# Gate work of an expert six units later, a third buffer for float32 weight parts, and row gathers placed behind GpSimd's subtractions

## Chip, cores and metric

One core of one Trainium2 chip runs the whole program as one kernel. The metric is the time of an execution on the device in microseconds (us); three executions of the kernel before gave 1203.83, 1204.12 and 1204.78 us, and their median is the time before.

## The reference

Three layers, one after the other, all in float32. The first takes the real part of a two-dimensional Fourier transform of x, four sequences of 2496 rows by 256. The second assigns the 9984 rows greedily to 8 experts of 1248 places each and applies the expert's two matrices. The third is a second mixture of experts, whose gate picks one expert for each row:

```python
# layer 2, N, D, E, F = 9984, 256, 8, 1024
for idx in argsort(-(x @ w_gate).flatten()):      # the best pairs first
    tok, e = idx // E, idx % E
    if assigned[tok] < 0 and counts[e] < N // E:
        assigned[tok] = e; counts[e] += 1
out[assigned == e] = relu(x[assigned == e] @ w1[e]) @ w2[e]
# layer 3
e_idx  = argmax(x @ w_gate2); gate_w = softmax(x @ w_gate2)[e_idx]
eom    = sigmoid(x @ w_output_gate)[e_idx]
out[e_idx == e] = gate_w * eom * (relu(x[e_idx == e] @ w1b[e]) @ w2b[e])
```

## The kernel before

**Numbers.** Every float32 matrix product is made of three float16 matmuls: a value is split into a high and a low half ("hi" and "lo"), and hi·hi, hi·lo and lo·hi are summed. So each weight block and each activation is split by two instructions: ScalarE (ACT) writes the high half, and VectorE (DVE) or GpSimd (POOL) subtracts it from the float32 value.

**Stages.** The Fourier transform and the choice of the first expert take the start. Then follow layer 2's experts 0 to 7, one after the other, in the trace from about 160 to 733 us, and layer 3 from about 754 us to the end. The change concerns layer 2 alone. Experts are chosen one at a time by a bisection on DVE with small matmuls (tiles `s_msk`, `sp`, `r`), which runs beside the expert before.

**One expert of layer 2.** Its 1248 rows come in three chunks (384, 384 and 480 rows). `hidden` (L898) makes, for each of 8 blocks of 128 hidden features, six matmuls into a PSUM tile `ph` (three buffers), then the relu on ACT (`ht`, L904), then the low half: on DVE (L910), or, for odd blocks in experts 0 to 4, ACT writes `hf` (L907) and POOL subtracts (L908). `out_block` (L915) makes 24 matmuls for 128 rows into `py` (two buffers), and ACT copies it to `yr` (L921). TensorE (PE) takes the hidden part of chunk c+1 before the output part of chunk c.

**Side work.** A class `Flow` emits the PE units of the experts in order and counts a clock of units, each about 1 us of PE's work. Between units it steps side generators when their due time has come: `yield 4.0` means "four units later". The order of the program on PE follows this. On the other engines a scheduler sets the final order, and `issue_after(x)` makes an instruction stand behind x on its queue. The generators that matter here:

- `prepare` (L1041): loads the six float32 weight blocks of an expert (`wf`, 0.5 MB each, issued on SP, the queue of SyncE; four stage buffers), finds the places of its rows (`places`, DVE L669 to L686, PE `px`), gathers the rows with ten indirect DMAs (`xg`, POOL L873; one buffer), and transposes the first chunk.
- `weights` (L1061): splits four of these blocks (ACT L783, DVE L785 or POOL L788).
- `gates` (L1074): uses the last two blocks, the second matrix transposed (`moe_w2t`), to multiply layer 3's gate columns into the expert's second matrix. It works in four steps of 256 columns: splits into `wt` (L799, one buffer), waits `GG` units, 12 matmuls (L809), two writes into `wh` (L815).
- `keep2` (L1082): prepares layer 3's weights while layer 2 runs. For each of 8 experts it takes four parts of 0.5 MB: SP loads a part into one of two float32 buffers (tiles `g_0`, `g_1`), ACT and DVE split it into `wp` (L1102, L1103), SP stores it (`wsd`, L1104), then the load of the part after next is issued. One part is due every 7 units (`KY`); a counter of experts (`KEEP`) holds it back. Parts are numbered 0 to 31 here.
- `rest` and `route` (L924): after an expert, layer 3's gate for its rows, the store `yd`, and ten indirect DMAs that scatter entries into a list (`lst`, POOL L985), four units apart.

SP's queue is in order: the loads of `wf`, which wait for a stage buffer, the store `yd`, which waits for the route, `keep2`'s loads and its stores all stand in it, one behind the other.

Of the kernel before, what the change touches and what calls it, by code (L numbers as in the profile page):

```python
# [723 lines left out]
GA = 0  # L724
G0 = 2.5
GN = 256
GG = 8.0
RY = 5.0
GY = 2.0
SY = 2.5  # L730
XY = 2.0
KY = 7.0
# [103 lines left out]
class Moe1:  # L836
    CH = ((0, 3), (3, 3), (6, 4))

    def __init__(self, tc, nc, a, xd, yd, lst, wsd, sel, pools, consts, bufs):
        self.tc, self.nc, self.a, self.xd, self.yd, self.lst, self.sel = tc, nc, a, xd, yd, lst, sel  # L840
        self.P = pools
        self.c = consts
        p = pools["keep"]
        self.base = p.tile([128, 8], F32, name="m_base")
        nc.vector.tensor_copy(self.base, consts["eoff"])
        self.wg = p.tile([128, 2, 2, 16], F16, name="m_wg")
        self.scat = []
        self.W = Weights(nc, pools["wts"], pools["stage"], a["moe_w1"], a["moe_w2"], a["moe_w2t"])
        self.wsd, self.bufs = wsd, bufs
        self.W2 = Weights(nc, pools["wts"], pools["stage"], a["moe2_w1"], a["moe2_w2"])  # L850
# [10 lines left out]
    def load(self, k):  # L861
        e = self.nc.sync.value_load(self.sel.ei[0:1, k:k + 1], min_val=0, max_val=7)
        return self.W.load(e)

    def gather(self, k):
        nc = self.nc
        idx = self.sel.idx[k]
        xg = self.P["xg"].tile([128, 10, D], F32, name="xg")

        def steps():  # L870
            for t in range(10):
                m = 128 if t < 9 else 96
                nc.gpsimd.indirect_dma_start(out=xg[:m, t], out_offset=None, in_=self.xd,  # L873
                                             in_offset=bass.IndirectOffsetOnAxis(ap=idx[:m, t:t + 1], axis=0))
                yield
        return xg, steps()

# [20 lines left out]
    def hidden(self, xt, n, wh, k):  # L898
        nc = self.nc
        ht = self.P["ht"].tile([128, 2, 8, 512], F16, name="ht")  # L900
        for fk in range(8):
            ph = self.P["psum"].tile([128, 512], F32, name="ph", bufs=3)
            ffn1_unit(nc, xt, wh[0], fk, n, ph[:, :n])
            self.act = nc.scalar.activation(ht[:, 0, fk, :n], ph[:, :n], AF.Relu)  # L904
            if fk % 2 and fk // 2 < HP[k]:
                hf = self.P["work"].tile([128, 480], F32, name="hf", bufs=HFB)
                nc.scalar.activation(hf[:, :n], ph[:, :n], AF.Relu)  # L907
                nc.gpsimd.tensor_sub(ht[:, 1, fk, :n], hf[:, :n], ht[:, 0, fk, :n])  # L908
            else:
                nc.vector.scalar_tensor_tensor(ht[:, 1, fk, :n], ph[:, :n], 0.0, ht[:, 0, fk, :n],  # L910
                                               op0=OP.max, op1=OP.subtract)
            yield n * 6 / 2400.0
        self.ht = ht
# [10 lines left out]
    def route(self, yr, k):  # L924
# [54 lines left out]
        nc.vector.tensor_copy(pi, px)  # L979
        nc.vector.tensor_add(self.base, self.base, pr[:, 80:88])  # L980
        self.counted = k
        ent = self.lst.rearrange("r (s w) -> (r s) w", w=2)
        for t in range(10):
            m = 128 if t < 9 else 96
            s = nc.gpsimd.indirect_dma_start(out=ent, in_=en[:m, t], in_offset=None,  # L985
                                             out_offset=bass.IndirectOffsetOnAxis(ap=pi[:m, t:t + 1], axis=0))
            for o in self.scat:
                self.tc.declare_no_dep(s.ins, o.ins, reason="every row has a place of its own")
            self.scat.append(s)
            yield 2.0 if k == 6 else 8.0 if k == 7 else 4.0  # L990

    def ffn(self, k, flow):

        wh = self.ws.pop(k)
        xg, xt = self.xgs.pop(k)
        yr = self.P["yr"].tile([128, 10, YW], F32, name="yr")
        self.nc.gpsimd.memset(yr[96:128, 9], 0.0)
        hts, nxt = {}, []

        def unit(d):  # L1000
            flow.unit(d)
            while nxt and nxt[0][0] <= 0:
                if next(nxt[0][1], 1):
                    nxt.pop(0)
                    self.cut += 1
                break
            if nxt:
                nxt[0][0] -= 1

        for c in range(4):  # L1010
            if c < 3:
                cur = xt
                if c < 2:
                    xt, st = self.xt(xg, c + 1)
                    nxt.append([3, st])
                for d in self.hidden(cur[0], cur[1], wh, k):
                    unit(d)
                hts[c] = self.ht
            else:
                self.tail = k  # L1020
            if c > 0:
                flow.until(lambda: self.gated >= k)
                t0, nt = self.CH[c - 1]
                for t in range(nt):
                    m = min(128, CAP - (t0 + t) * 128)
                    for d in self.out_block(hts[c - 1], t0 + t, t * 128, m, wh, yr):
                        unit(d)

        def rest():
            yield from self.route(yr, k)  # L1030
            self.routed = k
        flow.add(rest(), 1.0, prio=PR)
# [8 lines left out]
    def prepare(self):  # L1041

        for k in range(8):
# [4 lines left out]
                self.sel.placed = k  # L1048
            yield lambda: self.sel.placed >= k
            xg, steps = self.gather(k)  # L1050
            for t, _ in enumerate(steps):
                yield 0.0 if t < 4 else GY
            yield lambda: self.tail >= k - 1
            xt, steps = self.xt(xg, 0)
            for _ in steps:
# [1 line left out]
            self.xgs[k] = (xg, xt)  # L1057
            yield lambda: k in self.ws
            self.ready = k

    def weights(self):  # L1061

# [11 lines left out]
    def gates(self):  # L1074

        for k in range(8):
            yield lambda: k in self.gs and self.at >= (k - 1 if k else GA)
            for d in self.W.gate(*self.gs.pop(k), self.wg, self.P["psum"]):
                yield d or 0.0 if k else G0
            self.gated = k  # L1080

    def keep2(self):  # L1082
# [1 line left out]
        nc = self.nc  # L1084
        yield lambda: self.at >= KEEP[0]
        h = self.P["wts"].tile([128, 4, 2, 1024], F16, name="wp", bufs=1)
        fs = [self.bufs[q % 2].rearrange("p a b -> p (a b)")[:, :1024] for q in range(4)]

        def load(e, q):
            with self.tc.issue_after(self.W.at.ins):  # L1090
                self.W2.part(fs[q], slice(e, e + 1), q)

        load(0, 0)
        load(0, 1)
        for e in range(8):
            if e and KEEP[e] > self.at:
                yield lambda: self.at >= KEEP[e]
            else:
                yield KY
            for q in range(4):  # L1100
                with self.tc.issue_after(self.act.ins):
                    nc.scalar.activation(h[:, q, 0], fs[q], AF.Copy, scale=64.0)  # L1102
                nc.vector.scalar_tensor_tensor(h[:, q, 1], fs[q], 64.0, h[:, q, 0], op0=OP.mult, op1=OP.subtract)  # L1103
                nc.sync.dma_start(self.wsd[e, :, q], h[:, q])  # L1104
                if e < 7 or q < 2:
                    load(e + q // 2, (q + 2) % 4)
                if q < 3:
                    yield KY
            self.kept = e

    def run(self, flow, m2):
        self.cut = 0
        self.gated = -1
        self.counted = self.kept = -1
# [430 lines left out]
```

## Time and profile before

| what | value |
|---|---|
| median of three executions | 1204.12 us (1203.83 to 1204.78) |
| profiled execution, its own time | 1203.47 us |
| profiled execution, span from first to last instruction | 1201.7 us |
| mean granted clock of TensorE | 0.976 of full speed |
| busy share of the span | PE 93%, DVE 61%, POOL 41%, ACT 37% |

The span and the profiled execution's own time are 1.8 us apart, and the median of the three runs is 0.65 us above the profiled execution. A granted clock of 1 is 2.4 GHz, 0.5 is 1.2 GHz. In the rows below, `L824` is line 824 of the program; `py<-wh,ht` names the output tile and the inputs without buffer numbers; `x6` stands for six such instructions in a row.

### The profile page before, as it was taken

How to read it: one execution, taken by the hardware profiler on the slowest of the kernel's cores; microseconds unless marked ns; L12 is line 12 of the kernel's file. 1: busy time of each engine (PE TensorE's matmuls, PEld its weight loads, DVE VectorE, ACT ScalarE, POOL GpSimd, SP SyncE). 2: the span in 40 equal slices, each digit the busy share in tenths (PEclk: the TensorE clock that was granted, in tenths of full speed). 3: DMA queues.
4: the chain of work that ended last, by engine and by line, in shares of the span. 5: the costliest groups of instructions: out<-in, count | busy, mean ns of one | idle time of the engine just before them, and what ended most of it. 6: DMA issues, size and time to landing. Idle time of an engine off the chain costs nothing.

```text
span 1201.7 us, 24544 instructions
## 1 busy us (share of the span) xinstructions
PE 1119.0 (93%) x9823; PEld 821.8 (68%) x9823; DVE 729.9 (61%) x1786; ACT 440.8 (37%) x936; POOL 498.4 (41%) x471
## 2 busy tenths in 40 slices
PE   7998879979898989899798999999999999999998
PEld 4653546756667657567485767766766799999997
DVE  5866779897978977867456574434334343434343
ACT  3423334263452734345354443222223122222221
POOL 3825351468373781433306045643332334343331
PEclk8999989999999999989899999999999999999999
DMA  7834722243341571686838458444343366788782
GB/s 257 334 122 157 264 80 88 61 128 65 106 90 64 155 182 56 150 271 155 239 129 244 162 134 295 139 157 153 119 172 114 119 250 234 273 311 331 308 332 92
DMA packets 80036, 212.96 MB, mean 177 GB/s; under 512 B 11850, under 2 KB 48986, under 8 KB 69168
## 3 DMA queue, kind: packets, MB, share of 16 engines
q1 hardware_dynamic: 65360, 180.46, 44.5%
q0 software_dynamic: 14560, 30.91, 8.5%
q8 instruction: 78, 1.28, 0.5%
q14 instruction: 38, 0.31, 0.1%
HBM read 162.22 MB, written 50.42 MB: 177 GB/s over the span
## 4 chain that ended last, share of the span: by engine, by line
PE 28%; issue 23%; DVE 16%; POOL 10%; DMA 9%; ACT 2%; POOLq 0%; SPq 0%; DVEq 0%; ACTq 0%
PE py L832 14%; PE ph L824 9%; DMA g<-moe_w 6%; DMA out<-ot,tbrow 3%; POOL xg L1336 3%; POOL out L1381 2%; POOL g L1336 2%; DVE s_msk L525 2%; DVE ht L910 2%; PE px L693 1%; POOL xg L873 1%; DVE wp L1103 1%; PE pt L890 1%; POOL lst L985 1%; PE sp L531 1%
## 5 line engine op out<-in xcount | busy, mean ns | idle before, releaser
L832 PEld LDWEIGHTS <-ht 128*128 128x128 f16 (+1 forms) x3912 | 380.6, 99 | 61.3 <-issue 6.0
L824 PE MATMUL ph<-xt,wh 128*128 128x384 f16 (+4 forms) x2352 | 386.1, 316 | 26.9 <-DVE ht L910 14.8
L832 PE MATMUL py<-wh,ht 128*128 128x272 f16 (+2 forms) x3264 | 393.8, 277 | 4.2 <-ACT yr L921 4.2
L824 PEld LDWEIGHTS <-wh 128*128 128x128 f16 x2352 | 211.2, 99 | 148.8 <-issue 38.8
L1368 ACT ACTIVATE ht<-ph 128x512 f16<-128x512 f32 x166 | 99.1, 597 | 315.8 <-PE ph L824 315.8
L1369 DVE SCALAR_TENSOR_TENSOR ht<-ph,ht 128x512 f16<-128x512 f32 x166 | 114.8, 691 | 126.7 <-ACT ht L1368 126.7
L985 POOL DMA_INDIRECT lst<-r_en,r_pi x80 | 87.5, 1094 | 145.5 <-DVE r_pi L979 89.5
L904 ACT ACTIVATE ht<-ph 128x384 f16<-128x384 f32 (+1 forms) x192 | 98.4, 516 | 85.0 <-PE ph L824 76.9
L1381 POOL DMA_INDIRECT out<-ot,tarow x54 | 54.5, 1010 | 158.8 <-DVE ot L1380 152.1
L873 POOL DMA_INDIRECT xg<-xd,s_idx x80 | 87.9, 1099 | 34.9 <-issue 20.8
L910 DVE SCALAR_TENSOR_TENSOR ht<-ph,ht 128x384 f16<-128x384 f32 (+1 forms) x147 | 85.0, 585 | 19.4 <-ACT ht L904 19.1
L908 POOL TENSOR_TENSOR ht<-hf,ht 128x384 f16<-128x384 f32 (+1 forms) x45 | 48.7, 1090 | 93.2 <-ACT hf L907 80.0
L305 PE MATMUL big<-y,tab 128*128 128x36 f16 (+3 forms) x660 | 79.4, 273 | 1.1 <-DVE y L256 1.1
L921 ACT ACTIVATE yr<-py 128x272 f32<-128x272 f32 x80 | 31.3, 394 | 121.0 <-PE py L832 103.6
L832 PE MATMUL py<-wp,ht 128*128 128x256 f16 x648 | 73.7, 273 | 0.0
L824 PE MATMUL ph<-xt,wp 128*128 128x256 f16 (+2 forms) x624 | 72.9, 277 | 0.0
L1381 POOL DMA_INDIRECT out<-ot,tbrow x29 | 28.9, 997 | 101.9 <-DVE ot L1380 96.1
L1380 DVE TENSOR_SCALAR ot<-py,g 128x256 f32<-128x256 f32 x45 | 21.7, 483 | 70.6 <-PE py L832 70.6
L824 PEld LDWEIGHTS <-wp 128*128 128x128 f16 x624 | 51.4, 98 | 19.1
L1103 DVE SCALAR_TENSOR_TENSOR wp<-g,wp 128x1024 f16<-128x1024 f32 x32 | 39.9, 1247 | 32.2 <-ACT wp L1102 32.1
L305 PEld LDWEIGHTS <-tab 128*128 128x128 f16 x660 | 38.8, 97 | 30.0 <-issue 3.0
L525 DVE SCALAR_TENSOR_TENSOR s_msk<-s_vv,lo,s_jw 128x1280 f16<-128x1280 f32 x35 | 57.5, 1643 | 0.8
(254 smaller groups left out, 1313.2 us busy)
## 6 DMA issues: line engine op xcount, KB each, us to landing
wh<-wsd SPq DMA_DIRECT2D x50, 1024.0 KB, 6.0
wp<-wsd SPq DMA_DIRECT2D x26, 1024.0 KB, 6.0
wf<-moe_w SPq DMA_DIRECT2D x32, 512.0 KB, 6.0
g<-moe_w SPq DMA_DIRECT2D x32, 512.0 KB
wsd<-wp SPq DMA_DIRECT2D x32, 512.0 KB, 5.1
xa<-xa SPq DMA_DIRECT2D x8, 1280.0 KB, 11.1
xd<-xr SPq DMA_DIRECT2D x20, 512.0 KB, 4.8
yd<-yr SPq DMA_DIRECT2D x8, 1156.5 KB
```

The source lines that it names most:

```text
L305: self.nc.tensor.matmul(dst, self.tabs[par][k][:, cs, c, u], self.y[par][:, cs, w, c, bs, qs], start=(n == 0), stop=(n == 3 * NCH - 1))
L525: nc.vector.scalar_tensor_tensor(m, self.vv[:, :, None].to_broadcast(sh), lo, self.jw[:, r, None, :].to_broadcast(sh), op0=OP.subtract, op ...
L824: Flow.pe = nc.tensor.matmul(dst, w1[:, dk, a, fk * 128:fk * 128 + 128], xt[:, b, dk, :n], start=(k == 0), stop=(k == 5))
L832: Flow.pe = nc.tensor.matmul(dst, ht[:, a, fk, t0:t0 + m], w2[:, fk // 4, b, fk % 4], start=(fk == 0 and a == 0 and b == 0), stop=(fk == 7 ...
L873: nc.gpsimd.indirect_dma_start(out=xg[:m, t], out_offset=None, in_=self.xd, in_offset=bass.IndirectOffsetOnAxis(ap=idx[:m, t:t + 1], axis=0))
L904: self.act = nc.scalar.activation(ht[:, 0, fk, :n], ph[:, :n], AF.Relu)
L910: nc.vector.scalar_tensor_tensor(ht[:, 1, fk, :n], ph[:, :n], 0.0, ht[:, 0, fk, :n], op0=OP.max, op1=OP.subtract)
L985: s = nc.gpsimd.indirect_dma_start(out=ent, in_=en[:m, t], in_offset=None, out_offset=bass.IndirectOffsetOnAxis(ap=pi[:m, t:t + 1], axis=0))
L1336: nc.gpsimd.indirect_dma_start(out=g[:, h], out_offset=None, in_=self.yd, in_offset=bass.IndirectOffsetOnAxis(ap=row[:, 0, u + h:u + h + 1 ...
L1368: nc.scalar.activation(hi, src, AF.Relu)
L1369: nc.vector.scalar_tensor_tensor(lo, src, 0.0, hi, op0=OP.max, op1=OP.subtract)
L1381: st = nc.gpsimd.indirect_dma_start(out=self.out, in_=ot, in_offset=None, out_offset=bass.IndirectOffsetOnAxis(ap=row[:, 1, u + h:u + h + ...
```

## The change

Five edits, all within layer 2:

1. **Gates.** `GG`, the distance of a gate step's matmuls from its splits, is 6 units where it was 8, and an expert's gate work starts `GW` = 6 units later for experts 1 to 7.
2. **A third float32 buffer** `k_2` for `keep2`. Loads run three parts ahead where they ran two, and the load is issued on SP ahead of the part's store where it was behind it.
3. **Behind the subtractions.** Every gather and scatter is issued behind the last subtraction that the program has put on POOL up to there.
4. **Gathers in two goes.** For experts 1 to 7 three gathers come first, 2 units apart; the other seven come from a generator of their own, 3 units apart (2 for expert 1), and the transposes of chunks 1 and 2 are emitted only when all ten gathers are.
5. **Scatters.** Those of experts 0 to 5 begin 7 units later (`SD`) and stand 3.5 units apart where they stood 4.

```diff
-GG = 8.0
+GG = 6.0
+GW = 6.0
+GL = 3.0
+SD = 7.0
...
+    def behind(self):
+        return self.tc.issue_after(self.sub.ins) if self.sub else ExitStack()
...
-                nc.gpsimd.indirect_dma_start(out=xg[:m, t], out_offset=None, in_=self.xd,
-                                             in_offset=bass.IndirectOffsetOnAxis(ap=idx[:m, t:t + 1], axis=0))
+                with self.behind():
+                    nc.gpsimd.indirect_dma_start(out=xg[:m, t], out_offset=None, in_=self.xd,
+                                                 in_offset=bass.IndirectOffsetOnAxis(ap=idx[:m, t:t + 1], axis=0))
...
-                nc.gpsimd.tensor_sub(ht[:, 1, fk, :n], hf[:, :n], ht[:, 0, fk, :n])
+                self.sub = nc.gpsimd.tensor_sub(ht[:, 1, fk, :n], hf[:, :n], ht[:, 0, fk, :n])
...
+        if k < 6:
+            yield SD
...
-            yield 2.0 if k == 6 else 8.0 if k == 7 else 4.0
+            yield 2.0 if k == 6 else 8.0 if k == 7 else 3.5
...
+                    flow.until(lambda: self.got[k] == 10)
                     xt, st = self.xt(xg, c + 1)
...
-            for t, _ in enumerate(steps):
-                yield 0.0 if t < 4 else GY
+            self.got[k] = 0
+            if k:
+                for _ in range(3):
+                    next(steps)
+                    yield GY
+                self.flow.add(self.others(k, steps), GL)
+            else:
+                for t, _ in enumerate(steps):
+                    yield 0.0 if t < 4 else GY
+                self.got[k] = 10
...
+    def others(self, k, steps):
+        for t in range(3, 10):
+            next(steps)
+            self.got[k] = t + 1
+            yield GL if k > 1 else GY
...
+            if k:
+                yield GW
             for d in self.W.gate(*self.gs.pop(k), self.wg, self.P["psum"]):
...
-        fs = [self.bufs[q % 2].rearrange("p a b -> p (a b)")[:, :1024] for q in range(4)]
+        fs = [t.rearrange("p a b -> p (a b)")[:, :1024] for t in self.bufs]
+        fs.append(self.P["keep"].tile([128, 1024], F32, name="k_2", bufs=1))
...
+                if n < 29:
+                    load(n + 3)
                 nc.sync.dma_start(self.wsd[e, :, q], h[:, q])
-                if e < 7 or q < 2:
-                    load(e + q // 2, (q + 2) % 4)
```

Where the instructions stand on the engines' queues follows at three places; line numbers behind the change are those of the changed program.

**POOL, expert 3.** `lst` are the scatters of expert 2, `xg` the gathers of expert 4's rows, which the trace shows from 426 to 440 us, `ht<-hf,ht` the subtractions. Before:

```order
L908 TENSOR_TENSOR ht<-hf,ht 128x384
L985 DMA lst<-r_en,r_pi 81920x2 x2
L788 TENSOR_TENSOR wh<-wf,wh 128x2x256
L985 DMA lst<-r_en,r_pi 81920x2
L908 TENSOR_TENSOR ht<-hf,ht 128x384
L985 DMA lst<-r_en,r_pi 81920x2 x2
L873 DMA xg<-xd,s_idx_90 128x256 x8
L908 TENSOR_TENSOR ht<-hf,ht 128x384
L873 DMA xg<-xd,s_idx_90 128x256
L908 TENSOR_TENSOR ht<-hf,ht 128x384
L873 DMA xg<-xd,s_idx_90 96x256
```

After:

```order
L916 TENSOR_TENSOR ht<-hf,ht 128x384 x2
L791 TENSOR_TENSOR wh<-wf,wh 128x2x256
L881 DMA xg<-xd,s_idx_90 128x256 x3
L916 TENSOR_TENSOR ht<-hf,ht 128x384
L996 DMA lst<-r_en,r_pi 81920x2
L1008 MEMSET yr 32x272
L916 TENSOR_TENSOR ht<-hf,ht 128x384
L881 DMA xg<-xd,s_idx_90 128x256
L996 DMA lst<-r_en,r_pi 81920x2
L881 DMA xg<-xd,s_idx_90 128x256 x2
```

Ahead of a subtraction stood eight gathers at one place; now three at most do, and the scatters stand among the later gathers.

**ACT, the end of expert 5's hidden part.** `ht` is the relu, `yr` the copy of an output block, `wt` the second half of a gate's transposed block, `wp` a part of `keep2`, with the buffer from which it is read (`g_0`, `g_1`, `k_2`). Before:

```order
L904 ACTIVATE ht_7996<-ph_8077 128x384
L904 ACTIVATE ht_7996<-ph_8088 128x384
L799 ACTIVATE wt_8173<-wf_7671 128x256
L1102 ACTIVATE wp_5713<-g_1_2073 128x1024
L921 ACTIVATE yr_7767<-py_8103 128x272
L1102 ACTIVATE wp_5713<-g_0_2072 128x1024
L921 ACTIVATE yr_7767<-py_8131 128x272
L921 ACTIVATE yr_7767<-py_8160 128x272
L904 ACTIVATE ht_8196<-ph_8197 128x480
L1102 ACTIVATE wp_5713<-g_1_2073 128x1024
L904 ACTIVATE ht_8196<-ph_8206 128x480
```

After:

```order
L802 ACTIVATE wt_8227<-wf_7672 128x256
L912 ACTIVATE ht_7993<-ph_8062 128x384
L900 ACTIVATE xt_7992<-pt_8055 128x480
L912 ACTIVATE ht_7993<-ph_8071 128x384
L912 ACTIVATE ht_7993<-ph_8083 128x384
L1134 ACTIVATE wp_5718<-k_2_5719 128x1024
L1134 ACTIVATE wp_5718<-g_0_2072 128x1024
L929 ACTIVATE yr_7784<-py_8097 128x272
L929 ACTIVATE yr_7784<-py_8127 128x272
L929 ACTIVATE yr_7784<-py_8156 128x272
L912 ACTIVATE ht_8188<-ph_8189 128x480
```

Before, parts 13, 14 and 15 stood here, each with relus or copies behind it; now two parts (14 and 15) stand here together, part 13 stands earlier, and the gate's split stands three relus earlier than it did.

**DVE, expert 1.** `pi`, `pa`, `ha`, `hb` are the search for the places of the next expert's rows, `ht` the low half behind a relu. Before:

```order
L525 SCALAR_TENSOR_TENSOR s_msk_80<-s_vv_81,s_lo0_77,s_jw_85 128x1280
L669 CAST pi_3567<-pos_3529 128x80
L910 SCALAR_TENSOR_TENSOR ht_3382<-ph_3584,ht_3382 128x384
L670 TENSOR_SCALAR pi_3567<-pi_3567 128x80
L671 TENSOR_SCALAR pi_3567<-pi_3567 128x80
L673 CAST pa_3571<-pi_3567 128x80
L674 CAST pa_3571<-pi_3567 128x80
L677 TENSOR_TENSOR ha_3574<-ch_75,pa_3571 128x1600
L686 TENSOR_TENSOR hb_3578<-iob_1199,pa_3571 128x1280
L679 TENSOR_TENSOR ha_3574<-ha_3574,ch_75 128x1600
L910 SCALAR_TENSOR_TENSOR ht_3382<-ph_3605,ht_3382 128x384
```

After:

```order
L669 CAST pi_3567<-pos_3529 128x80
L525 SCALAR_TENSOR_TENSOR s_msk_80<-s_vv_81,s_lo0_77,s_jw_85 128x1280
L670 TENSOR_SCALAR pi_3567<-pi_3567 128x80
L671 TENSOR_SCALAR pi_3567<-pi_3567 128x80
L673 CAST pa_3571<-pi_3567 128x80
L674 CAST pa_3571<-pi_3567 128x80
L677 TENSOR_TENSOR ha_3574<-ch_75,pa_3571 128x1600
L686 TENSOR_TENSOR hb_3578<-iob_1199,pa_3571 128x1280
L679 TENSOR_TENSOR ha_3574<-ha_3574,ch_75 128x1600
L918 SCALAR_TENSOR_TENSOR ht_3382<-ph_3584,ht_3382 128x384
L918 SCALAR_TENSOR_TENSOR ht_3382<-ph_3605,ht_3382 128x384
```

The low half of `ph_3584` stood behind one of the search's instructions and now stands behind eight of them.

## Rows read from the trace of the kernel before

**Rows 1.** Windows: length, busy PE, PEld, DVE, ACT, POOL; granted clock, DMA share, GB/s.

```profile
235.00:735.00 500.00, 452.38 (x3871) 324.31 (x3870) 365.49 (x990) 233.90 (x512) 228.10 (x209) 0.97 0.52 150
735.00:1200.00 465.00, 459.12 (x4022) 367.88 (x4020) 188.88 (x370) 121.40 (x217) 167.56 (x165) 1.00 0.57 208
```

**Rows 2.** Waits of PE, 235 to 735 us: total us, times, longest.

```profile
PE ph L824 <- DVE ht L910: 14.2, 6, 6.6
PE ph L824 <- ACT hf L907: 10.2, 3, 5.4
```

**Rows 3.** Waits of ACT in the same stretch.

```profile
ACT wp L1102 <- DMA g<-moe_w: 40.2, 17, 8.3
ACT hf L907 <- POOL ht L908: 7.7, 2, 5.3
```

**Rows 4.** Chain that ended last, 490 to 590 us: start, us, what.

```profile
497.08 13.69 DMA g<-moe_w
...
571.71 11.78 DMA g<-moe_w
```

**Rows 5.** Timeline at expert 4: start, us, instruction, [idle before <- releaser].

```profile
506.54 1.06 ACT L1102 ACTIVATE wp<-g 128x1024 f16<-128x1024 f32 x1 [4.99 <-DMA g<-moe_w]
...
510.79 1.06 ACT L1102 ACTIVATE wp<-g 128x1024 f16<-128x1024 f32 x1 [2.45 <-DMA g<-moe_w]
...
512.82 2.56 PE L824 MATMUL ph<-xt,wh 128*128 128x480 f16 x6 [5.43 <-ACT hf L907]
```

**Rows 6.** Timeline at expert 5, PE and ACT.

```profile
578.50 1.38 PE L824 MATMUL ph<-xt,wh 128*128 128x480 f16 x6 [1.62 <-DVE ht L910]
...
583.51 1.06 ACT L1102 ACTIVATE wp<-g 128x1024 f16<-128x1024 f32 x1 [8.32 <-DMA g<-moe_w]
...
586.45 4.96 PE L824 MATMUL ph<-xt,wh 128*128 128x480 f16 x12 [6.58 <-DVE ht L910]
...
591.57 2.77 PE L824 MATMUL ph<-xt,wh 128*128 128x480 f16 x12
```

**Rows 7.** The four half-clock stretches spoken of, as in rows 1.

```profile
373.80:376.90 3.10, 3.08 (x16) 2.10 (x17) 2.08 (x8) 0.00 (x0) 0.00 (x0) 0.50 0.00 0
441.80:445.20 3.40, 3.40 (x12) 1.40 (x11) 2.70 (x10) 2.33 (x7) 2.94 (x3) 0.50 0.44 160
512.80:516.80 4.00, 3.98 (x11) 1.62 (x11) 3.05 (x11) 1.46 (x3) 3.26 (x3) 0.50 0.93 289
586.40:591.90 5.50, 5.45 (x25) 2.25 (x25) 3.01 (x4) 1.97 (x3) 0.00 (x0) 0.50 0.59 207
```

**Rows 8.** Timeline at expert 6.

```profile
644.66 2.94 PE L832 MATMUL py<-wh,ht 128*128 128x272 f16 x24 [2.46 <-ACT yr L921]
```

**Rows 9.** Timeline at expert 3, POOL and PE.

```profile
426.29 3.02 POOL L873 DMA_INDIRECT xg<-xd,s_idx  x1 [0.30 <-issue]
...
440.70 0.56 PE L824 MATMUL ph<-xt,wh 128*128 128x480 f16 x2 [3.79 <-ACT hf L907]
```

**Rows 10.** Timeline at expert 2.

```profile
368.17 3.20 POOL L908 TENSOR_TENSOR ht<-hf,ht 128x480 f16<-128x480 f32 x3
368.31 1.01 DVE L669 CAST pi<-pos 128x80 int32<-128x80 f32 x1
...
373.82 0.19 PE L542 MATMUL sp<-r,ch 128*128 128x8 f16 x1 [3.07 <-DVE r L538]
```

**Rows 11.** Timeline at expert 1.

```profile
255.45 0.19 DVE L669 CAST pi<-pos 128x80 int32<-128x80 f32 x1
...
256.15 1.14 PE L824 MATMUL ph<-xt,wh 128*128 128x384 f16 x6 [3.64 <-DVE ht L910]
256.48 0.99 DVE L677 TENSOR_TENSOR ha<-ch,pa 128x1600 f16<-128x1600 f16 x1
```

**Rows 12.** Timeline of PE at expert 0's start.

```profile
156.55 0.33 PE L890 MATMUL pt<-cf,xg 128*128 128x128 f32 x1 [1.27 <-DMA xg<-xd,s_idx]
159.55 0.48 PE L890 MATMUL pt<-cf,xg 128*128 128x128 f32 x1 [2.66 <-DMA xg<-xd,s_idx]
```

More of the change, by code (lines that the diff above doesn't have):

```diff
@@ L846, in __init__ @@
         self.wg = p.tile([128, 2, 2, 16], F16, name="m_wg")
-        self.scat = []
+        self.scat, self.sub = [], None
         self.W = Weights(nc, pools["wts"], pools["stage"], a["moe_w1"], a["moe_w2"], a["moe_w2t"])
@@ L984, in route @@
             m = 128 if t < 9 else 96
-            s = nc.gpsimd.indirect_dma_start(out=ent, in_=en[:m, t], in_offset=None,
-                                             out_offset=bass.IndirectOffsetOnAxis(ap=pi[:m, t:t + 1], axis=0))
+            with self.behind():
+                s = nc.gpsimd.indirect_dma_start(out=ent, in_=en[:m, t], in_offset=None,
+                                                 out_offset=bass.IndirectOffsetOnAxis(ap=pi[:m, t:t + 1], axis=0))
             for o in self.scat:
@@ L1086, in keep2, with load @@
         h = self.P["wts"].tile([128, 4, 2, 1024], F16, name="wp", bufs=1)
-        fs = [self.bufs[q % 2].rearrange("p a b -> p (a b)")[:, :1024] for q in range(4)]
-        def load(e, q):
+        fs = [t.rearrange("p a b -> p (a b)")[:, :1024] for t in self.bufs]
+        fs.append(self.P["keep"].tile([128, 1024], F32, name="k_2", bufs=1))
+        def load(n):
             with self.tc.issue_after(self.W.at.ins):
-                self.W2.part(fs[q], slice(e, e + 1), q)
-        load(0, 0)
-        load(0, 1)
+                self.W2.part(fs[n % 3], slice(n // 4, n // 4 + 1), n % 4)
+        for n in range(3):
+            load(n)
         for e in range(8):
@@ L1100, in keep2 @@
             for q in range(4):
+                n = 4 * e + q
+                f = fs[n % 3]
                 with self.tc.issue_after(self.act.ins):
-                    nc.scalar.activation(h[:, q, 0], fs[q], AF.Copy, scale=64.0)
-                nc.vector.scalar_tensor_tensor(h[:, q, 1], fs[q], 64.0, h[:, q, 0], op0=OP.mult, op1=OP.subtract)
+                    nc.scalar.activation(h[:, q, 0], f, AF.Copy, scale=64.0)
+                nc.vector.scalar_tensor_tensor(h[:, q, 1], f, 64.0, h[:, q, 0], op0=OP.mult, op1=OP.subtract)
+                if n < 29:
+                    load(n + 3)
                 nc.sync.dma_start(self.wsd[e, :, q], h[:, q])
-                if e < 7 or q < 2:
-                    load(e + q // 2, (q + 2) % 4)
                 if q < 3:
@@ L1111, in run @@
     def run(self, flow, m2):
+        self.got, self.flow = {}, flow
         self.cut = 0
```

## Prediction

> **What bounds the kernel.** I read the busy time by stretch first [rows 1]. From 735 us on PE is busy 459.12 of 465.00 us at full clock, and no edit touches that layer but through the moment at which it starts. From 235 to 735 us, experts 1 to 7 of layer 2, PE is busy 452.38 of 500.00 us: 47.6 us stand idle there, and some of the 452.38 are spent at half the granted clock. So any gain or loss is PE's idle time in this stretch, plus what the clock takes behind a pause.
>
> Next I read what ended those pauses. The two largest groups [rows 2] have matmuls of the hidden part waiting for the low half on DVE (14.2 us in 6 times, 6.6 at most) and for `hf` on ACT (10.2 us in 3 times, 5.4 at most). Neither names the cause; the engine named has a wait of its own in front. ACT's waits [rows 3] give two: the parts of `keep2`, for whose loads ACT stood 40.2 us in 17 times, up to 8.3 us, and POOL's subtraction (5.3 us once). ACT takes its queue in order, so relus behind a part that has not landed wait with it, and PE waits for the relus. The chain of work that ended last [rows 4] shows the loads themselves as links: 13.69 us from issue to landing at 497.08, 11.78 us at 571.71.
>
> Last I read the timeline at the pauses. The places that the change can reach, with PE's pause in each:
>
> - Expert 4, 512.82 us: 5.43 us. ACT waited 4.99 us for one part, let a relu through, and waited 2.45 us for the next [rows 5].
> - Expert 5, 578.50 and 586.45 us: 1.62 and 6.58 us; ACT waited 8.32 us for one part [rows 6].
> - Expert 6, 644.66 us: 2.46 us behind a copy `yr` on ACT [rows 8].
> - Expert 3, 440.70 us: 3.79 us. A subtraction stood on POOL behind eight gathers, the first of them at 426.29 [rows 9], and `hf` with its three buffers waited for it.
> - Expert 2, 373.82 us: 3.07 us, in the choice of the next expert; DVE was late with `r` [rows 10].
> - Expert 1, 256.15 us: 3.64 us behind DVE's low half [rows 11].
>
> **What half the clock costs.** Four of these pauses are followed by a stretch in which the granted clock is 0.50, so 1.2 GHz [rows 7]. In the last, twelve matmuls took 4.96 us; the same twelve took 2.77 us just behind it [rows 6]. That is 2.2 us lost in 5.5 us of the stretch, 0.4 of its length. By that share the other three lose 1.2 us (of 3.10, expert 2), 1.4 (of 3.40, expert 3) and 1.6 (of 4.00, expert 4).
>
> **Part by part.**
>
> *Third buffer, expert 4.* SP's queue stands still at an expert's end, behind the next expert's weight loads and the store `yd`. Before, part 6 was the first issued behind that block, and part 7 was issued at 497.08 [rows 4]. With three buffers part 6 is issued ahead of it, and part 7 takes part 6's slot. It would land where part 6 did, about 506.5, so ACT is through with it at 507.6 where it was through at 510.79 + 1.06 = 511.85 [rows 5]: the relus behind it come 4.2 us earlier. Forecast −4.2; bounds 0 (ACT stands for another load as long) and −7.0 (5.43 and 1.6 of clock).
>
> *Third buffer, expert 5.* Part 15 was issued at 571.71 and landed at 583.49 [rows 4]; ACT took it at 583.51. Three parts ahead, it is issued ahead of its neighbours' splits, and SP puts the gate's load and parts ahead of the store. The whole is 1.62 + 6.58 + 2.2 = 10.4 us. Parts 14 and 15 now stand back to back on ACT ahead of the copies, as the order shows, and a wait for the first of them remains; I leave a pause of the smaller size, 1.5. Forecast −8.9; bounds 0 and −10.4.
>
> *Third buffer, expert 6.* Of 2.46 us I leave 0.7. Forecast −1.8; bounds 0 and −2.5.
>
> The Trainium skill says in "SBUF — State Buffer", section "Summary: rules for kernel authors", to estimate an HBM transfer end to end at about 358 GB/s. By that page a part of 0.5 MB would take an estimated 1.5 us, two buffers would be ample and the third worth nothing; the sum would lose 14.9 us and come to −3.0, 1201. The trace does not agree: 13.69 and 11.78 us from issue to landing [rows 4].
>
> *Gathers behind subtractions, expert 3.* Before, eight gathers stood ahead of a subtraction; now at most three, with others behind it. The pause of 3.79 and 1.4 us of clock can go whole. Forecast −5.2; bounds 0 and −5.2.
>
> *The same, expert 2.* Three subtractions ran in a row for 3.20 us, and DVE's cast of 128 x 80 beside them took 1.01 us [rows 10], where the same cast took 0.19 in expert 1 [rows 11]. Three of the search's small operations stand there in a row, so some 3 x 0.8 = 2.4 us of the pause are this contention. In the new order the subtractions come one by one and earlier. A pause of 1.0 stays: 3.07 − 1.0 + 1.2 gives −3.3; bounds 0 and −4.3.
>
> *DVE, expert 1.* The low half of `ph_3584` now stands behind seven further instructions of the search: two of the 128 x 1600 form (0.99 each), one of 1280 columns (0.8 by size), four small ones of 0.19 [rows 11]: 3.5 us. Before, it stood ahead of them and PE still paused 3.64 us. The search itself gets done earlier, and PE's side matmuls with it. Forecast +2.0; bounds 0 and +4.9 (3.5 and 1.4 of clock, the share 0.4 of one more stretch of 3.4 us).
>
> *Gates, scatters, counts.* The gate's matmuls and splits keep their number; so do gathers and scatters (80 each), `keep2`'s loads and stores (32 each). The gate of an expert is due 2 units earlier than before at its end, and it must be done before the expert's first output block; PE has other units meanwhile. Nothing by itself: what hides it is the hidden part of the first two chunks. If that cover is gone it is in the rival on late gathers or in the next term.
>
> *What is late next.* ACT, DVE and POOL are closely filled beside PE, and a pause that goes uncovers the one behind it. The kernel's smaller pauses are 1.3 to 2.7 us [rows 6, 8, 12]. Five places are mended; I take half of a small pause of 1.5 at each, 5 × 0.7 = +3.5; bounds 0 and +7.5.
>
> Sum: −4.2 − 8.9 − 1.8 − 5.2 − 3.3 + 2.0 + 3.5 = −17.9. The sum is made against the profiled execution, 1203.47 us: 1185.6. The median of the runs lies 0.65 above that execution, so about 1186.
>
> **Rivals.**
>
> *The buffer yields little* (1198). The block on SP's queue stays as long as it was, so the first part behind it lands no earlier than before, and ACT waits the same time for part 7 that it waited for part 6. Then only the two terms of POOL and the one of DVE count: −5.2 − 3.3 + 2.0 = −6.5, 1197.6 at the median. For it: at expert 4 the parts wait for SP, not for a buffer. Against: with three ahead one part less is issued behind the block, and at expert 5 the late part was not the first behind it.
>
> *Nothing late next* (1175). All the pauses go with their clock: −7.0 − 10.4 − 2.5 − 5.2 − 4.3 = −29.4, 1174.7. Against: PE's pauses here are many and small, and an in-order ACT has a next one ready.
>
> *Late gathers, slower* (1212). A gather that has not landed stops PE in its transposes: at expert 0's start 1.27 and 2.66 us [rows 12], 3.9 a chunk. The seven later gathers now come 3 units apart and stand on POOL among scatters and behind subtractions. If the chunks 1 and 2 of an expert both met this, it would cost 7.9 us an expert; three experts make 23.6, which is more than 17.9, and give 1210, four 1218. It decides from the third expert on. Against: the first gather of an expert starts well ahead of the expert's own start (426.29, and the change delays the last by some 21 units at most), and the view of PE's waits [rows 2] has no group of transposes that wait for `xg`.
>
> The Trainium skill speaks against the change at this point: "SBUF — State Buffer", section "SBUF: two separate sides", says that GpSimd writes a gather's descriptors through a port pair shared with VectorE, which an instruction of VectorE that uses both ports holds to its end, so gathers spread among such work would be issued late. The trace has one gather that took 3.02 us on POOL [rows 9], which agrees with it, and shows none that held up PE in this stretch.
>
> *It does not do what it says* (1204). Three buffers, but the same part is late, and the subtractions wait on ACT anyway: no change.
>
> **Chances and range.** The forecast of 1186 has 0.50, with 1178 to 1194 as its own range (half of the third buffer's terms either way). The buffer that yields little has 0.24, nothing late next 0.10, late gathers 0.10, no change 0.06. The range 1174 to 1203 leaves out the slower rival, most of no change, and the tail below the third. A measurement of this kernel tells about 0.2%, 2.4 us, from no change. Faster by more: 0.84; the same: 0.06; slower: 0.10.
>
> **What would show it.** Right: no wait of ACT over 5 us for a part, `hf` never over 2 us behind POOL, pauses at expert 5 under 3 us in all, and no half-clock stretch in experts 3 and 5; expert 1 some 2 us longer. Wrong: ACT's total wait for parts still near 40 us (the second case), or transposes of experts 2 to 5 waiting for `xg` (the slower case).

## The result and the profile after

Six executions of the changed kernel on the first chip have a median of 1189.71 us (1188.47 to 1194.72), six of the kernel before 1203.97; the ratio is 0.9895, with a 95% interval of 0.9873 to 0.9917. That is 14.3 us by the medians, 10.0 to 15.3 by the interval. A ratio here and below leaves out executions more than 1.5% above the fastest of their kernel; a median is that of all. The forecast was 1186 in a range of 1174 to 1203, so time, sign and range held. Its parts did not all hold.

Windows of the changed kernel, the stretch of experts 1 to 7 and the rest (columns as in [rows 1]), then two pieces of expert 5 and a stretch at half clock there:

```profile
232.00:720.00 488.00, 448.20 (x3878) 324.35 (x3876) 361.40 (x993) 234.44 (x514) 238.69 (x209) 0.98 0.56 153
720.00:1187.00 467.00, 459.97 (x4028) 368.86 (x4028) 188.94 (x370) 121.63 (x217) 167.46 (x165) 1.00 0.57 209
...
547.00:570.00 23.00, 22.30 (x148) 14.23 (x147) 17.21 (x30) 9.43 (x18) 14.32 (x16) 1.00 1.04 217
570.00:590.00 20.00, 10.25 (x81) 7.74 (x80) 7.34 (x10) 6.87 (x12) 6.10 (x6) 0.76 0.93 351
...
580.30:590.50 10.20, 4.41 (x20) 2.99 (x20) 2.27 (x4) 1.63 (x3) 0.00 (x0) 0.50 0.80 300
```

PE stands idle for 39.8 us of the first stretch, where it was 47.6 [rows 1]; in the rest it is idle for 7.0 us, where it was 5.9. Waits of PE, then of ACT, in that stretch:

```profile
PE py L835 <- ACT yr L929: 12.9, 3, 9.8
PE ph L827 <- DVE ht L918: 7.0, 2, 6.7
PE sp L542 <- DVE r L538: 4.6, 5, 1.6
PE ph L827 <- ACT hf L915: 4.0, 2, 3.8
```

```profile
ACT wp L1134 <- DMA g<-moe_w: 20.8, 6, 4.8
ACT wp L1134 <- DMA k<-moe_w: 2.1, 1, 2.1
```

ACT's wait for parts is little more than half of what it was [rows 3], 22.9 us in 7 waits against 40.2 in 17. ACT's wait for POOL's subtraction is gone from the view. But PE now has one pause of 9.8 us behind the copy `yr`; the longest of that stretch was 6.6 before [rows 2]. The pauses that answer to [rows 5, 6, 8, 10, 11], on PE's timeline:

```profile
258.06 4.00 PE L827 MATMUL ph<-xt,wh 128*128 128x384 f16 x12 [6.75 <-DVE ht L918]
...
370.41 0.18 PE L542 MATMUL sp<-r,ch 128*128 128x8 f16 x1 [1.64 <-DVE r L538]
...
499.56 2.56 PE L827 MATMUL ph<-xt,wh 128*128 128x480 f16 x6 [3.77 <-ACT hf L915]
...
586.09 5.10 PE L835 MATMUL py<-wh,ht 128*128 128x272 f16 x24 [9.75 <-ACT yr L929]
...
633.12 2.94 PE L835 MATMUL py<-wh,ht 128*128 128x272 f16 x24 [2.55 <-ACT yr L929]
```

How long each expert took, from the end of the tenth and last copy `yr` of the expert before to the end of its own tenth. By the trace expert 7 ends at 739.3 us before, not at 733, and at 725.3 after:

| expert | before | after | difference | forecast for the place |
|---|---|---|---|---|
| 1 | 79.1 | 79.4 | +0.3 | +2.0 |
| 2 | 75.2 | 71.8 | −3.4 | −3.3 |
| 3 | 78.0 | 74.3 | −3.7 | −5.2 |
| 4 | 72.9 | 70.2 | −2.7 | −4.2 |
| 5 | 73.2 | 73.6 | +0.4 | −8.9 |
| 6 | 65.3 | 63.2 | −2.0 | −1.8 |
| 7 | 58.6 | 58.0 | −0.5 | 0 |
| to expert 0's end | 237.1 | 234.7 | −2.4 | 0 |

The last line is hardly the change's: up to there PE's order differs only in twelve small matmuls of one gate step, 24 matmuls later than before. The profiled execution of after held full clock from 13.69 to 153.64 us, where that of before had stretches at half clock; the fastest kernel of the last group below, whose order up to there is that of before, had them again and came to expert 0's end at 236.9 us.

### The profile page after: what moved, and what is told of

Same layout as the page of the kernel before. It is cut to its first block, busy times and chain, and to the rows that moved or that the text cites. A ratio compares the mean times of both kernels' runs of the same rounds, so it can differ in the third digit from the quotient of the medians.

```text
span 1187.3 us, 24540 instructions
## 1 busy us (share of the span) xinstructions
PE 1109.4 (93%) x9823; PEld 818.8 (69%) x9823; DVE 723.7 (61%) x1786; ACT 440.7 (37%) x936; POOL 512.1 (43%) x471
## 4 chain that ended last, share of the span: by engine, by line
PE 35%; issue 20%; DVE 15%; DMA 9%; POOL 7%; ACT 2%; POOLq 0%; SPq 0%; DVEq 0%; ACTq 0%
PE py L835 17%; PE ph L827 13%; DMA g<-moe_w 5%; DMA out<-ot,tbrow 3%; POOL out L1414 2%; POOL xg L1369 2%; DVE s_msk L525 2%; POOL g L1369 2%; DVE ht L918 2%; PE px L693 2%; PE pt L898 1%; DVE wt L803 1%; DVE wp L1135 1%; DVE hb L686 1%; PE sp L531 1%
## 5 line engine op out<-in xcount | busy, mean ns | idle before, releaser
L835 PEld LDWEIGHTS <-ht 128*128 128x128 f16 (+1 forms) x3912 | 381.2, 99 | 70.2 <-issue 13.9
L881 POOL DMA_INDIRECT xg<-xd,s_idx x80 | 92.3, 1154 | 35.7 <-issue 19.0
L916 POOL TENSOR_TENSOR ht<-hf,ht 128x384 f16<-128x384 f32 (+1 forms) x45 | 54.6, 1213 | 90.2 <-ACT hf L915 77.5
L835 PE MATMUL py<-wp,ht 128*128 128x256 f16 x648 | 73.7, 273 | 0.0
L827 PE MATMUL ph<-xt,wp 128*128 128x256 f16 (+2 forms) x624 | 72.9, 277 | 0.0
L1413 DVE TENSOR_SCALAR ot<-py,xg 128x256 f32<-128x256 f32 x38 | 18.4, 483 | 58.5 <-PE py L835 58.5
## 6 DMA issues: line engine op xcount, KB each, us to landing
xa<-xa SPq DMA_DIRECT2D x8, 1280.0 KB, 11.7
```

Source lines behind the costliest of these rows:

```text
L827: Flow.pe = nc.tensor.matmul(dst, w1[:, dk, a, fk * 128:fk * 128 + 128], xt[:, b, dk, :n], start=(k == 0), stop=(k == 5))
L835: Flow.pe = nc.tensor.matmul(dst, ht[:, a, fk, t0:t0 + m], w2[:, fk // 4, b, fk % 4], start=(fk == 0 and a == 0 and b == 0), stop=(fk == 7 ...
L916: self.sub = nc.gpsimd.tensor_sub(ht[:, 1, fk, :n], hf[:, :n], ht[:, 0, fk, :n])
```

## What expert 5 shows

ACT's timeline in the changed kernel, part 7 at expert 4, then four parts (16 to 19) at expert 5 and the copies behind them:

```profile
496.79 1.06 ACT L1134 ACTIVATE wp<-g 128x1024 f16<-128x1024 f32 x1 [4.58 <-DMA g<-moe_w]
...
570.30 1.06 ACT L1134 ACTIVATE wp<-g 128x1024 f16<-128x1024 f32 x1 [2.86 <-DMA g<-moe_w]
...
573.19 1.06 ACT L1134 ACTIVATE wp<-k 128x1024 f16<-128x1024 f32 x1 [0.45 <-DVE ht L918]
578.17 1.06 ACT L1134 ACTIVATE wp<-g 128x1024 f16<-128x1024 f32 x1 [3.93 <-DMA g<-moe_w]
...
584.70 1.06 ACT L1134 ACTIVATE wp<-g 128x1024 f16<-128x1024 f32 x1 [4.77 <-DMA g<-moe_w]
585.66 0.66 ACT L929 ACTIVATE yr<-py 128x272 f32<-128x272 f32 x2
```

And the loads in the chain that ended last:

```profile
551.06 19.21 DMA g<-moe_w
...
572.64 11.95 DMA g<-moe_w
```

Part 16 was issued at 551.06, well ahead of its use, and landed 19.21 us later; part 19 was issued when 16 had been split, and took 11.95 us. In the windows above, the DMA engines are busy all the time from 547 to 570 us (share 1.04) and move 217 GB/s. From 546.8 to 560.1 us SP issued five parts, three stores of parts and the store `yd`, 5.5 MB in all; at 217 GB/s that is an estimated 25 us of transfers, and parts 16 and 18 took 19 us among them. So three parts ahead are about as many as land in the time in which ACT's queue takes four, and the copies `yr` stand behind the fourth.

## The experiments

Three groups of runs, on three more chips. The chip of the last group runs the kernel before in 1204.0 us, as the first chip did; the two others take 1279.6 and 1278.5 us for it. Ratios are to the kernel before on the same chip, with 95% intervals.

**Pieces alone, on a chip of 1279.6 us.** The buffer alone, its core:

```diff
+        fs.append(self.P["keep"].tile([128, 1024], F32, name="k_2", bufs=1))
...
+                if n < 29:
+                    load(n + 3)
                 nc.sync.dma_start(self.wsd[e, :, q], h[:, q])
-                if e < 7 or q < 2:
-                    load(e + q // 2, (q + 2) % 4)
```

> Only the third float32 buffer and the load ahead of the store; gates, gathers and scatters as before. Theory A, by the terms of the prediction, the buffer is the larger half: expert 4's pause at 512 falls by 4.2 us, expert 5's two pauses by 8.9, expert 6's by 1.8, so 11 to 15 us less than before, 1189 to 1193. Theory B, by the trace of the whole change, where expert 5 took as long as before: the buffer is worth 4 to 5 us at experts 4 and 6 and nothing at expert 5, 1199 to 1200, and the pauses at 440 and 373 us stay (3.8 and 3.1 us).

Measured: 0.9998 (0.9971 to 1.0026), nothing, which neither theory had. The loads are less late. ACT's waits for parts, those without a named releaser included:

```profile
ACT wp L1105 <- issue: 4.1, 2, 2.4
ACT wp L1105 <- DMA k<-moe_w: 4.0, 1, 4.0
ACT wp L1105 <- DMA g<-moe_w: 3.0, 2, 1.8
```

That is 11.1 us; in the other three kernels of this group, which have two buffers, it is 24.0, 20.4 and 29.1 us. So the waits are about half as long with the buffer, as far as kernels that differ in other edits too can tell, and PE did not gain by that here.

POOL's edits alone, as a diff to the changed kernel (the load goes back behind the store as well):

```diff
-GG = 6.0
-GW = 6.0
+GG = 8.0
...
-        fs.append(self.P["keep"].tile([128, 1024], F32, name="k_2", bufs=1))
```

> Only the gathers and scatters behind the subtractions, in two goes and with the later scatters; two buffers and the gates as before. Theory A: the pauses at 440 us (expert 3) and 373 us (expert 2) go, 7 to 8.5 us less than before, 1195.5 to 1197, and expert 5's pause of 6.6 us stays. Theory B, the same at experts 2 and 3 and nothing elsewhere: experts 2 and 3 are 3.4 and 3.9 us shorter as in the whole change. Rival: POOL's order frees ACT only with the buffer there too, and the time stays within 2.4 us of 1204.

Measured: 0.9942 (0.9909 to 0.9976), 7.4 us by the ratio and 5.2 by the medians, as theories A and B said; the time can't tell them apart. The gate edit alone:

```diff
-GG = 8.0
+GG = 6.0
+GW = 6.0
...
+            if k:
+                yield GW
```

> Only the gate's 6 units of delay and its steps of 6 units. Theory A: nothing of its own but DVE's order in expert 1, where the low half stands behind the search for places: the pause at 256 us grows from 3.6 to 6 or 7 us with half the clock behind it, 2 to 4 us more than before, 1206 to 1208. Rival: the moved split of the gate frees ACT at expert ends, up to 3 us a place, and the time falls below 1201.

Measured: 1.0056 (1.002 to 1.0092), 7 us slower by the ratio, where 2 to 4 were expected; the interval reaches from 2.6 to 11.8. The whole without the buffer (its diff is the first of these, undone in the changed kernel):

> The whole change but for the third buffer: two buffers and the load behind the store, as before. Theory A: the buffer's terms come back, 11 to 15 us above the changed kernel, 1200 to 1204, with ACT's total wait for parts back near 40 us. Theory B: 4 to 5 us above it, about 1194, with experts 4 and 6 alone longer.

Measured: 0.9985 (0.9954 to 1.0016): the gain of POOL's edits and the loss of the gate's, about added.

**The whole and two mends, on a chip of 1278.5 us.** The changed kernel itself:

> The changed kernel itself, as a measure for the other three of this call. If the pieces measured singly (buffer 1.000, GpSimd 0.994, gates 1.006, GpSimd and gates 0.9985 of before) add up on their chip, the whole is within 0.5% of before there; on a chip like the first it is 0.987 to 0.992. Theory A: the buffer's worth depends on the rest being fast, since PE must be ahead of the loads for a part to be late.

Measured: 0.9943 (0.9905 to 0.9981), half of the first chip's gain; the medians of all executions, 1276.20 and 1278.48 us, are closer, 0.9982. Without the gate edit, as a diff to it:

```diff
-GG = 6.0
-GW = 6.0
+GG = 8.0
...
-            if k:
-                yield GW
```

> The changed kernel with the gates as before (steps of 8 units, no delay). Theory A: the gate's edit only costs, at expert 1 through the order on DVE: 3 to 7 us faster than the changed kernel, expert 1 itself 3 to 4 us shorter and its pause at 256 us back at 3.6. Rival: the gate's delay is needed beside the buffer at the ends of experts 4 to 6, where its splits stand ahead of relus; then expert 1 is shorter and experts 4 to 6 are longer by as much, and the time is the same within 3 us.

Measured: 0.9859 (0.9808 to 0.9911), so without the gate edit the kernel is 0.8% faster. The gate's old times for experts 0 and 1 alone:

```diff
-            if k:
+            if k > 1:
                 yield GW
...
-            for d in self.W.gate(*self.gs.pop(k), self.wg, self.P["psum"]):
+            for d in self.W.gate(*self.gs.pop(k), self.wg, self.P["psum"], GG if k > 1 else 8.0):
```

> The changed kernel with the old gate times for experts 0 and 1 alone. DVE's order at expert 1's place search is as before. Theory A: all of the gate's cost sits at expert 1: the same as without the gates' edit, 3 to 4 us under the changed kernel. Rival: the cost is spread over the later experts; then it is within 1.5 us of the changed kernel.

Measured: 0.9876 (0.9828 to 0.9924), like the one before it. So the cost of the gate edit comes with the first experts' gates. PE at the place search of expert 1, in the whole and in this kernel:

```profile
268.39 3.45 PE L827 MATMUL ph<-xt,wh 128*128 128x384 f16 x12 [6.75 <-DVE ht L918]
```

```profile
262.88 2.08 PE L827 MATMUL ph<-xt,wh 128*128 128x384 f16 x6 [4.18 <-DVE ht L918]
```

Expert 1 took 91.3 us in the whole and 87.3 here. Expert 2, however, took 74.1 and 77.5, and the two executions differ most at expert 6 (73.7 and 65.8). So the traces do not show where the 8.6 us between the two ratios are lost. Parts 16 to 19 twelve units apart:

```diff
-                    yield KY
+                    yield (12.0 if e == 4 else KY)
```

> The changed kernel with parts 16 to 19 of the prepared weights 12 units apart instead of 7; ACT's queue then has two of them, not four, between expert 5's last relus and its first copies behind the gate. Theory A: expert 5's pause (9.8 us on the first chip, behind waits of 3.9 and 4.8 us for these parts, which came 12 and 19 us after their issue) is one of loads that come too slowly for four parts in 15 us: it goes but for 2 us, and expert 5 is 5 to 8 us shorter, the later experts at most 2 us longer. Rival: the pause moves whole to the part that is next late, in expert 6, and the time stays within 2.4 us of the changed kernel.

Measured: 0.9958 (0.9919 to 0.9997), no different from the whole. In the profiled executions the pause of the whole at expert 5 is gone in this one, whose PE runs through there; at the start of layer 3 it has a pause of 4.33 us, where the whole has one of 3.71. The whole, then this one:

```profile
616.05 4.17 PE L835 MATMUL py<-wh,ht 128*128 128x272 f16 x21 [3.94 <-ACT yr L929]
```

```profile
612.86 1.55 PE L835 MATMUL py<-wh,ht 128*128 128x272 f16 x12
...
790.00 1.12 PE L1383 MATMUL pt<-cf,g 128*128 128x128 f32 x4 [4.33 <-DVE xt L1388]
```

Expert 5 took 67.2 us against 72.1 and expert 6 75.8 against 73.7. From expert 7's end to layer 3's first result (`out`) it was 31.1 us against 26.2, with the last part taken 18.8 us ahead of expert 7's end, not 32.7. But expert 7 itself took 62.7 us against 72.9, at a granted clock of 1.00 against 0.93, and the two profiled executions are 8.0 us apart where the kernels are not. So the spacing takes expert 5's pause away; where its gain is lost is not shown.

**Both mends and single pieces, on a chip of 1204.0 us.** Both mends, with ten units so that the last parts keep their place:

```diff
-            if k:
+            if k > 1:
                 yield GW
...
-            for d in self.W.gate(*self.gs.pop(k), self.wg, self.P["psum"]):
+            for d in self.W.gate(*self.gs.pop(k), self.wg, self.P["psum"], GG if k > 1 else 8.0):
...
-                    yield KY
+                    yield (10.0 if e == 4 else KY)
```

> The changed kernel with the old gate times for experts 0 and 1 and parts 16 to 19 ten units apart. With ten units the last parts stand on ACT where they stood in the changed kernel; with twelve they stood later, and layer 3 began 4.6 us later behind expert 7's end. Theory A: both mends add up, expert 1 is 3 to 4 us shorter, expert 5's pause of 4 us is gone and nothing is given back at layer 3's start: 0.980 to 0.985 of the kernel before. Rival: PE's own idle time without a releaser covers the parts on these chips, the spacing adds nothing, and it is 0.985 to 0.989, as with the old gate times alone.

Measured: 1186.04 us, 0.985 (0.9819 to 0.9881), the lowest of all. The same with two buffers:

```diff
-        fs.append(self.P["keep"].tile([128, 1024], F32, name="k_2", bufs=1))
-                if n < 29:
-                    load(n + 3)
                 nc.sync.dma_start(self.wsd[e, :, q], h[:, q])
+                if e < 7 or q < 2:
+                    load(e + q // 2, (q + 2) % 4)
```

> The first kernel of this call with two buffers and the load behind the store. Theory A: the third buffer is worth 5 to 10 us once POOL holds nothing up: 0.4 to 0.8% slower than the first kernel, and ACT's total wait for parts is 20 to 40 us against 5 to 15. Rival: the buffer is worth nothing on these chips, as it was alone (1.000): within 0.2% of the first kernel.

Measured: 1208.04 us, 1.0027 (1.0002 to 1.0052). The buffer, with its loads three ahead and ahead of the store, is worth 22.0 us by the medians here (0.985 / 1.0027 = 0.982), more than twice what was expected. With two buffers the kernel is no faster than the kernel before, though it has POOL's edits whole: experts 2 and 3 are 4.1 and 1.9 us shorter than before (on the first chip), expert 4 is 5.4 and expert 7 6.9 us longer. Pauses of PE at experts 4 and 5, with three buffers, then with two:

```profile
503.29 2.46 PE L827 MATMUL ph<-xt,wh 128*128 128x480 f16 x6 [3.35 <-ACT hf L915]
...
583.11 5.60 PE L835 MATMUL py<-wh,ht 128*128 128x272 f16 x24 [5.27 <-ACT yr L929]
```

```profile
500.50 2.56 PE L827 MATMUL ph<-xt,wh 128*128 128x480 f16 x6 [4.38 <-DVE ht L918]
...
525.80 0.55 PE L898 MATMUL pt<-cf,xg 128*128 128x128 f32 x3 [3.34 <-DVE wh L819]
...
582.21 7.91 PE L827 MATMUL ph<-xt,wh 128*128 128x480 f16 x24 [6.14 <-DVE ht L918]
```

And ACT's waits for parts from 460 to 610 us, in the same order:

```profile
ACT wp L1134 <- DMA g<-moe_w: 7.1, 3, 4.2
ACT wp L1134 <- DMA k<-moe_w: 5.9, 2, 3.8
```

```profile
ACT wp L1131 <- DMA g<-moe_w: 25.7, 8, 7.9
ACT wp L1131 <- issue: 4.2, 1, 4.2
```

From two buffers to three, experts 4 to 7 are 9.6, 5.6, 2.4 and 2.5 us shorter, 20.1 in all, and experts 1 to 3 are the same within 0.5. At expert 5 the ten units left 5.27 of the 9.75 us, and expert 5 took 68.9 us. Expert 7 took 62.9, though, 4.9 more than in the changed kernel, with a pause behind the list of layer 3's rows. The kernel with two buffers has it too, 4.89 us; the four kernels near 1204 us without the spacing (before, after and the next two) do not:

```profile
700.54 0.29 PE L1317 MATMUL pt<-cf,t_ls 54*128 54x54 f32 x1 [3.22 <-DMA t_ls<-lst,tali]
```

Only the rule that ties gathers and scatters behind the subtractions:

```diff
+                with self.behind():
...
+            with self.behind():
...
+                self.sub = nc.gpsimd.tensor_sub(ht[:, 1, fk, :n], hf[:, :n], ht[:, 0, fk, :n])
```

> Only the rule that gathers and scatters stand behind the last subtraction; their number, times and goes as before, two buffers, gates as before. Theory A: this rule alone is what moves POOL's order, since it is the only edit that ties it: 0.993 to 0.996 of before, and the pause at 440 us goes. Rival: without the second go eight gathers still stand in a row, now behind the subtraction but in front of the next expert's, and the time is within 0.2% of before.

Measured: 1.0046 (1.002 to 1.0071), slower. The pause at 440 us is gone, and expert 4's is longer, behind the same loads:

```profile
513.89 2.56 PE L824 MATMUL ph<-xt,wh 128*128 128x480 f16 x6 [7.58 <-ACT hf L912]
```

```profile
ACT wp L1108 <- DMA g<-moe_w: 38.0, 14, 8.9
```

Only the spread gathers and later scatters, without that rule:

```diff
+            if k:
+                for _ in range(3):
+                    next(steps)
+                    yield GY
+                self.flow.add(self.others(k, steps), GL)
...
+        if k < 6:
+            yield SD
```

> Gathers in two goes and later scatters, without the rule that ties them behind the subtractions; two buffers, gates as before. Theory A: the order on POOL is nearly that of before, eight gathers ahead of a subtraction: within 0.2% of before, the pause of 3.8 us in expert 3 stays. Rival: the later emission alone takes them out of the way: 0.993 to 0.996.

Measured: 0.9988 (0.9967 to 1.001), the same, as theory A said. POOL still held ACT up at expert 3, and PE waited for a copy behind that, for 2.07 us and not 3.8:

```profile
447.25 0.57 ACT L913 ACTIVATE hf<-ph 128x480 f32<-128x480 f32 x1 [7.17 <-POOL ht L914]
...
448.16 0.39 PE L834 MATMUL py<-wh,ht 128*128 128x272 f16 x2 [2.07 <-ACT yr L927]
```

## Why the prediction was right, point by point

- **The sum.** It came close partly by luck. The forecast was −17.9 us and the medians give −14.3, but the two profiled executions, whose spans differ by 14.4, have 2.4 of them ahead of expert 1. Experts 1 to 7 saved 11.7 us, and the largest term, expert 5, brought nothing.
- **The signs.** Held: no wait of ACT over 5 us for a part (4.77 at most), none behind POOL in the view, no half clock at expert 3. Not held: expert 5's pauses were to be under 3 us in all and there is one of 9.75, with 10.2 us at half clock; expert 1 was to be 2 us longer.
- **What bounds the kernel.** Right: what the change gains lies in PE's idle time and half-clock stretches of experts 1 to 7; layer 3 took the same (462.4 us from expert 7's last copy to the end before, 462.0 after).
- **Third buffer, expert 5.** This is the step that failed: −8.9 forecast, +0.4 measured. It took a part that is issued ahead for one that has landed, and looked for the wait at parts 14 and 15. Those waited 0.0 and 2.3 us. The late ones were parts 16, 18 and 19, whose loads took 12 to 19 us with the DMA engines full, and the pause moved from the relus to the copies `yr`. With these parts spaced, expert 5 is shorter on both kinds of chip (67.2 us for 72.1, and 68.9 where the changed kernel took 73.6 on the first chip), with no gain in the whole time from the spacing alone.
- **Third buffer, experts 4 and 6.** Mechanism right, −2.7 and −2.0 us against −4.2 and −1.8. The pause at expert 4 stayed at 3.77 us, behind a wait of 4.58 for part 7, about the wait that part 6 had before [rows 5].
- **The buffer's worth in all.** Mis-sized. The term counted what the change would save from the state before, 14.9 us less part of what comes late next. Between the two kernels of the last group, which have the two mends, it was 22.0 us: with the other edits in, two buffers cost more than they did before the change (expert 4 took 78.3 us with them, 72.9 before). The chips near 1279 us point the same way: the buffer alone brought nothing there (0.9998), but POOL's edits with it came to 0.9859 and without it, on the other of the two chips, to 0.9942. By the Trainium skill's figure for a transfer ("SBUF — State Buffer", section "Summary: rules for kernel authors"), an estimated 1.5 us for a part, the buffer would have been worth nothing. The traces do not agree with that: the parts issued at expert 5 took 6.0 to 19.3 us.
- **Gathers behind subtractions.** Right at experts 2 and 3 in the whole kernel (−3.4, −3.7 against −3.3, −5.2); at expert 3 the choice's small waits (1.47 us and less) came out behind the pause. That at most three gathers stand ahead of a subtraction there does not hold: in the trace four gathers and three scatters do.

```profile
416.86 1.78 POOL L881 DMA_INDIRECT xg<-xd,s_idx  x1 [0.16 <-issue]
...
428.71 1.11 POOL L916 TENSOR_TENSOR ht<-hf,ht 128x480 f16<-128x480 f32 x1
```

That subtraction's `hf` was ready at 424.85 us, so it stood 3.9 us behind them, and neither ACT nor PE waited for it. As an edit by itself it is not shown to gain on a chip of 1204 us: the rule alone lost 0.46% and the spread alone gained nothing. Without the rule ACT still stood 7.17 us for the subtraction, and with the rule alone PE's pause passed to expert 4's loads. Both together, with two buffers and the two mends, lost 0.27%: what experts 2 and 3 won, experts 4 and 7 lost.

- **DVE at expert 1.** The pause grew by 3.1 us (3.64 to 6.75), within its bounds of 0 to 4.9, and half clock followed for 6.8 us where it was 3.4. Expert 1 as a whole lost 0.3 us only; in the last group's kernel with the old times of the first gates it took 79.3 us, the same. On the slower chips the edit cost 0.6% alone and 0.8% beside the others, with expert 1 4 us longer and expert 2 3 us shorter.
- **What is late next.** Too small. The terms ahead of it come to −21.4 us, and experts 1 to 7 together saved 11.7 in the profiled execution, so 9.7 were given back where 3.5 were allowed; 9.3 of them are expert 5's. It did not come in five small pieces but at one place.
- **The rivals.** *The buffer yields little* fell on a chip like the first, by the experiment with two buffers; the buffer alone was not tried there. *Nothing late next* and *no change* fell by the time. *Late gathers* fell too: no transpose of experts 1 to 7 waits for `xg` in the changed kernel's waits. The Trainium skill's rule that spoke for it ("SBUF — State Buffer", section "SBUF: two separate sides") may be behind the 0.95 to 2.05 us that the gathers took on POOL from 408 to 442 us, which no run here tests, nor does the one gather of 3.02 us show it; none of them held up PE.

Open: the buffer alone was not run on a chip of 1204 us, nor POOL's edits together without the gate's. The buffer and the load's place ahead of the store were never parted; in the changed kernel five stores of parts held SP for 0.55 to 1.50 us each from 552 to 577 us, small beside 22.0. On a chip of 1279 us the buffer alone gave nothing and POOL's edits gave 0.6%; near 1204 us the buffer gives most. Why the two kinds of chip differ was not settled.

## What to carry to other kernels

A buffer more helps by the landing time of its load against the time in which the consuming queue takes the others: read the landing under the load of that stretch, not its issue. An engine that takes its queue in order turns one late load into a wait of everything behind it, so look at what stands behind the load's consumer, and keep it from being what TensorE needs next. And run edits on a queue's order together with the resource they compete for: here the order rule alone lost 0.5% and the spread alone gave nothing, the buffer alone gave nothing on another chip, and together they gave 1%.

## What was not expected of the hardware

The same program took 1204 us on two chips and 1279 us on two others. On the slower ones TensorE has short pauses without a releaser, most of them in layer 2, and half-clock stretches in layer 3, where the others have none. The windows of layer 3, the changed kernel on the chip of 1278.5 us, then on the first, and last the largest group of pauses without a releaser on the former, from 240 to 1270 us:

```profile
802.00:1270.00 468.00, 452.17 (x3890) 358.01 (x3888) 172.25 (x290) 113.22 (x203) 153.67 (x151) 0.98 0.55 198
```

```profile
742.00:1180.00 438.00, 437.68 (x3873) 353.88 (x3872) 171.76 (x286) 114.02 (x202) 157.64 (x155) 1.00 0.58 212
```

```profile
PE py L835 <- issue: 11.4, 17, 1.7
```

In that window PE was idle 15.8 us of 468, on the first chip 0.3 us of 438. Of the 11.4 us without a releaser 10.1 lie ahead of 790 us; in the window the largest group is behind the relus on ACT, 8.3 us in 6 times. What a change is worth was different too, so a piece should be priced on the kind of chip on which the whole is.
